# Re-searching a static instruction order with lengths measured from the trace

## The chip, the cores and the metric

The kernel runs on one core of one Trainium2 chip. The metric is device time in microseconds (us) of one execution. Three runs of the kernel before gave 1224.88, 1224.0 and 1226.82 us, median 1224.88. A profiled execution has a span of 1222.5 us from its first instruction to its last.

The engines are named as in the profile: PE multiplies matrices (PEld is its weight load), DVE and ACT do elementwise work, reductions and activations, POOL does slower elementwise work, SP only issues transfers. Each engine takes its instructions strictly in the order in which the program lists them, and waits where an operand or a buffer is not there yet. So the order in each engine's list decides how much of one engine's latency lies beside another's work.

## The reference

A random-feature attention for 8 batches of 8 heads is followed by a Fourier-mixing block with a two-layer network, all in float32:

```python
def phi(x):                                    # q and k, scaled
    h = einsum('bhsd,md->bhsm', x, omega) - sum(x*x)/2
    return exp(h - max(h)) / sqrt(m)
kv  = einsum('bhsm,bhsd->bhmd', k_p, v)        # per head: 128 features x 64
out = (q_p @ kv) / (q_p @ sum(k_p) + 1e-6)     # 8 x 8 heads x 576 x 64
x   = out as (8, 576, 512)
u   = x + real(fft(fft(x, axis=1), axis=2))
un  = (u - mean(u)) / sqrt(var(u) + 1e-6)
y   = u + relu(un @ w_ch1) @ w_ch2             # 512 -> 2048 -> 512
```

The two weight matrices come as 64-bit floats; the kernel converts them on the chip.

## The kernel before

The program has two parts. The first does the attention (32 pairs of heads, each a stream of steps), the Fourier mixing of eight batches, the conversion of the weights in 32 slabs, and the network for the first four tiles of 128 rows ("plain"). The second does the network for the other 4096 rows in eight blocks of 512, with a scheme that saves products by adding blocks first.

Neither part is written in its final order. Each stream is a generator that yields a `Step` before it emits the instructions of that step. A step names its engine (or a choice of two), an assumed length, events that it needs and makes, and buffers that it takes and gives:

```python
RATE = 190.0      # KB per us of a transfer
HOP = 0.15        # from the end of a step to its reader on another engine
TURN = 0.1        # change of PE's array mode (whole, quarters, halves)

class Listing:
    def run(self, streams, picks=None):
        ...
        for item in todo if pick is None else [todo[int(pick, 36)]]:
            got = self.start(*item[2:])             # earliest begin, by the assumed lengths
            key = got[0] + item[2].bias, item[0]
            if best is None or key < best[0]:
                best = key, got, item
        ...
        end = begin + step.engines[eng]
        done = end + step.late + (HOP if eng != NONE else 0.0)
        if step.kb:
            self.moved = max(self.moved, end) + step.kb / RATE
```

The first part is run with `PICKS`, a string of 1919 characters: each says which of the waiting streams goes next. It was found by a search outside the kernel. The second part is run without picks: there the step that can begin first, by the assumed lengths and a small bias, goes next. Where a step has a choice of engines, the assumed lengths decide in both parts. All of this happens when the program is built; on the chip there is only the resulting list of each engine.

The steps of one pair of heads (attention), by their lines in this kernel:

```python
def attn(n):
    # L470  PE: transpose k,q (9 tiles)         -> L477 ACT: copy out (kqT)
    # L544  PE: projection, 64x64 quarters      -> L488 DVE: negated maximum (nmx)
    #                                           -> L505 ACT: exp, 18 x 128x128 (e)
    # L578  PE: kv product (36, quarters)       -> L592 DVE or L594 ACT: copy out (kv)
    # L470  PE: transpose e of q (9 tiles)      -> L477 ACT: copy out (qeT)
    # L621, L629  PE: numerator and denominator (20, halves)
    # L638-L641   DVE: add, reciprocal, multiply -> x
```

The mixing of a batch folds x (L668 to L694, DVE, some on POOL), multiplies with cosine and sine tables (L712, then L739 and L744 on PE), and adds the residual (L760 ACT, L765 to L777 DVE and POOL). A slab of weights goes through:

```python
def narrow(i, dst, raw):
    step = Step({ACT: 0.72, POOL: 1.4}, ...)      # L407 POOL or L409 ACT: scale
    yield Step(DVE, 0.43, port=True, bias=0.19)   # L411
    yield Step(DVE, 1.15, port=True, bias=0.36)   # L413, L416
    yield Step(DVE, 0.7, port=True, bias=-0.99)   # L418
    yield Step(POOL, 1.3, makes=("w", i), ...)    # L420
```

The plain network is L863 (transposes of the normalised tile), L924 (first layer), L910 or L908 (relu on ACT or DVE) and L947 (second layer, added up by L960). It needs converted weights and mixed batches, so it is the work that can fill PE's gaps once both are there. In the second part L1130 is the first layer, L1309 the second; w2 is summed beforehand by L1017, w1 by L1075.

Of the kernel before, what the change touches and what calls it, by code (L numbers as in the profile page):

```python
# [33 lines left out]
PE, ACT, DVE, POOL, SP, NONE = "pe", "act", "dve", "pool", "sp", "none"  # L34
# [3 lines left out]
RATE = 190.0  # L38
HOP = 0.15

TURN = 0.1
# [7 lines left out]
    "00e2ede0ebed3dedebfcdcddfeede3fdfhbi8cdefdebfdgafaggec9hddk0kiij2jejgj7lfffffhcdfffdfcggjehegfi7gjbl"  # L49
    "hbhkjgkkdihfhi7hci7bfiadgkhhjce9didbhhb7gggbfihbbf97acbhbeghefaie8bc7chhhcgfc7cedddh9dd1ccdfif8eggih"  # L50
    "f6g8ejihichdihidfkhfhgjckgigh6eihggiddebd6dcg9eei7cfhei6ddfgihhj78gmkmiidaggjfigdmlg6khhjcj6agghifgg"
    "kh6afejekjkjfigji6j8hjjjiilcj9iegcigdhllkmldjmkkf9j80lca5m7bdai6gfikjaljkika6lhjggic9feikeejhgjij5d7"
    "ldjeafedkdeikjje5g5ielfafej6egkicg8dffgikghjijiee7eeifaaeefhefehdeh7iffd6hb7eeidiedhggiijbkj35fjkjhk"
    "kfgfhkk3h795g4e4i6khchlijigkjji4hlfjfd8lfhlg4mi64bfgjjedjgibk6ijj5cgcijhicgi6lii9fi9lf6ggdijf6bgd8fe"
    "icddchifajihj9fgihgjgi6jbhi6degcbg48ffgfh6ii5kjigihf7jgf9ejggafji7gf7egdfh6ficd6dbhfeeh5addfh5be5bff"
    "c48gai8hg9ageefcj5j7gh6haeeghhjikiehi5mg6lghhl5jjhagd5nglkmlccnjldj9llj45lkjjaemh6gbmlf8f7hgekef6hke"
    "87cldljj8bkhihbhhdc6ffgadkdf7ad5kdbgjhhig6lgcel5mdjedilaidedejihgjegi5ggjhcf5dgc5c775kccdh489j8ddgff"
    "h8cbdgiejkkechjhkkki5gj7kgjjjjfjjjh4i7dhhjjfi4k4h4kjchehg6ihk975g5bfejcehg3dgmggiej6m55bf9igig5h66gg"
    "jjjfiieifh8ege5kdihdlhiheief9k5fimhmcio8hgk7fge5jhgdeifagbgbjeeekhgclgigh7ge8fgefddfaci4icdffhgfid8f"
    "gjffhgihd6gc6cjeelgf3af8hbiccgchgfebg5c9d6ehdfcfeeagghffbhc6f9egchggh6aeehfeekjccbdfafdf50h0gcgabgea"  # L60
    "7fcdcfabg6be8bd4c9dcdcdbcebe6bcgb6cefbacadfeaca7dcdcdchdf9abca66f8dcbd8b98c8aa9c8dd2eabcc87a7b758697"
    "a27277ba9688848aa89a99992b98aa9a287a888729d8a993ba8ac9788aede65bdaacb69ba8ba659b54387a986aaa9baccade"
    "ad9b7bfcecffffde79fe9e6h9bgc3gc3be1eac26e7ebeddbdfeefegd6cdfed2ddf3dadeb3e3cc9dc6c5dbbdcab7b3c72b79b"
    "acbb8abbb679a6a9bb9ab49c7b38a93caa998888888888899888686981458778888888888888841933648786583b59691776"
    "a7c67267761bb4bcb6cc9a679a8aaba3f94df49cbaa675793a9aa88778388a88a93995aa39b94a4954585536126424112222"
    "3333533555523346545266421330442216087635433437704543770334535754155544556455155414437756241426224444"
    "1112032232202111100"
# [39 lines left out]
class Listing:  # L107
# [24 lines left out]
    def start(self, step, ready, before):  # L132

        queued = before in step.engines and len(step.engines) == 1
        t = ready[0] if queued else ready[1]
        for ev in step.after:
            if ev not in self.made:
                return None
            t = max(t, self.made[ev])
        for name in set(step.take):  # L140
            if name in WIDTH:
                t = self.banks_at(WIDTH[name], t)[1]
                if t == math.inf:
                    return None
                continue
            free = sorted(self.buffers[name])
            n = step.take.count(name)
            if len(free) < n:
                return None
            t = max(t, free[n - 1])  # L150

        def begin(e):
            return max(t, self.free[e] if e != NONE else 0.0, self.free[PORT] if step.on_port(e) else 0.0)

        eng = min(step.engines, key=lambda e: begin(e) + step.engines[e])
        t = begin(eng)
        return t + (TURN if eng == PE and step.mode != self.mode else 0.0), eng

    def run(self, streams, picks=None):
# [17 lines left out]
        while todo:  # L177
# [20 lines left out]
            done = end + step.late + (HOP if eng != NONE else 0.0)  # L198
# [55 lines left out]
def kernel(  # L254
# [142 lines left out]
    def narrow(i, dst, raw):  # L397


        lo, hi = raw[:, :, 0], raw[:, :, 1]  # L400
        lof, hif, bits = lo.bitcast(F32), hi.bitcast(F32), dst.bitcast(U32)


        step = Step({ACT: 0.72, POOL: 1.4}, after=(("raw", i),), port=True, bias=1.11)
        yield step
        if step.eng == POOL:
            nc.gpsimd.tensor_scalar(dst, hif, 2.0**-112, None, op0=ALU.mult)  # L407
        else:
            nc.scalar.activation(out=dst, in_=hif, func=AF.Copy, scale=2.0**-112)  # L409
        yield Step(DVE, 0.43, port=True, bias=0.19)  # L410
        nc.vector.tensor_scalar(hi, hi, 0x80000000, None, op0=ALU.bitwise_and)  # L411
        yield Step(DVE, 1.15, port=True, bias=0.36)
        nc.vector.scalar_tensor_tensor(  # L413
            bits, bits, 3, hi, op0=ALU.logical_shift_left, op1=ALU.bitwise_or
        )
        nc.vector.tensor_scalar(hi, bits, 0xFF800000, None, op0=ALU.bitwise_and)  # L416
        yield Step(DVE, 0.7, port=True, bias=-0.99)
        nc.vector.scalar_tensor_tensor(lof, lo, 2.0**-52, hif, op0=ALU.mult, op1=ALU.mult)  # L418
        yield Step(POOL, 1.3, makes=("w", i), give=("slab",), port=True, bias=1.25)
        nc.gpsimd.tensor_tensor(out=dst, in0=dst, in1=lof, op=ALU.add)  # L420
# [23 lines left out]
    def first():  # L444

        yield Step(NONE, 3.0)
        yield Step(PE, 0.4, take=("bank",))
        b, omps = got()
        nc.tensor.transpose(omps[:, 0:128], om[:].rearrange("m i d -> m (i d)"), ident[:])
        yield Step(DVE, 0.3, makes="om2", give=(b,))  # L450
        nc.vector.tensor_scalar(om2[:], omps[:, 0:128], SCALE, None, op0=ALU.mult)

    def transposed(src, name, groups, after, makes, give, back=None):
# [3 lines left out]
        for j0, j1 in groups:  # L457
# [3 lines left out]
                0.11 * m,  # L461
# [12 lines left out]
    def evicted(dst, b, j0, j1, makes, back):  # L474
        yield Step(ACT, 0.15 + 0.115 * (j1 - j0), 0.1, makes=makes + (j0,), give=(b,), bias=0.08)
# [5 lines left out]
    def softmax(n, ts, num, b, es):  # L481
# [3 lines left out]
        yield Step(DVE, 0.15 + 0.27 * num, bias=-0.56)  # L485
# [10 lines left out]
        for i, one in enumerate(b):  # L496
            if num == 4 or not i:
                yield Step(
                    ACT, 1.18 if num == 4 else 0.65, 0.0, take=(size,),
# [12 lines left out]
    def attn(n):  # L512
# [16 lines left out]
        def pairs_of(js, *ts):  # L529
# [4 lines left out]
                0.235 * len(js),  # L534
# [52 lines left out]
        def keep():  # L587
            step = Step({DVE: 0.3, ACT: 0.35}, take=("kv",), give=(kvb,), makes=("kv", n))
# [20 lines left out]
            1.23,  # L609
# [24 lines left out]
        yield Step(DVE, 1.25, after=(("frame", b),), give=(ndb,), makes=("x", b, pr), bias=-0.07)  # L634
# [18 lines left out]
    def mix(b):  # L653
# [7 lines left out]
        def folds(n):  # L661
            op = (ALU.add, ALU.subtract)[n]
            even, odd = (ALU.subtract, ALU.add) if n else (ALU.add, ALU.subtract)
            step = Step({DVE: 1.22, POOL: 2.5} if n else DVE, 1.22, take=("half",), port=True)
# [4 lines left out]
            yield Step(DVE, 1.15, port=True, bias=-0.08)  # L669
# [3 lines left out]
            for dst, src in ((h[:, 0:NL], h[:, 0:NL]), (h[:, NL : NL + 1], x[:, 4:5])):  # L673
# [7 lines left out]
                {DVE: 1.2, POOL: 2.6} if n else DVE, 1.2,  # L681
# [18 lines left out]
        for n, (tab, name) in enumerate(((cs, "cs"), (cs, "cs"), (sn, "sn"), (sn, "sn"))):  # L700
# [19 lines left out]
            def kept(n=n, yb=yb, yp=yp):  # L720
                yield Step(ACT, 0.44, 0.1, makes=("y", b, n), give=(yb,), bias=0.1)
# [3 lines left out]
        for c in range(NC3):  # L725
# [3 lines left out]
                1.33,  # L729
# [23 lines left out]
    def residual(b, c, x, abb):  # L753
# [3 lines left out]
        yield Step(ACT, 0.4, 0.1, take=("bmp",), give=(b1,))  # L757
# [4 lines left out]
        for last, (dst, op) in enumerate(((mi, ALU.subtract), (pl, ALU.add))):  # L762
            yield Step(DVE, 0.67, give=(b0,) if last else (), bias=-0.1)
# [23 lines left out]
        yield Fork(summed(0, mi, pl, DVE, 0.85))  # L787
        if c < NL:
            yield from summed(1, pl, mi, POOL, 1.6)
# [54 lines left out]
    def norm_of(j, t, i, pool, dst):  # L844
# [7 lines left out]
        yield Step(DVE, 1.09, bias=-0.23)  # L852
# [3 lines left out]
        yield Step(POOL, 0.7, port=True, bias=-0.18)  # L856
        nc.gpsimd.tensor_tensor(rstd[:], rstd[:], mhalf[:], op=ALU.pow)  # L857
        yield Step(DVE, 0.56, port=True)
        nc.vector.tensor_scalar(u[:], u[:], mv[:, 0:1], rstd[:], op0=ALU.subtract, op1=ALU.mult)
        yield Step(PE, 0.45, take=("bank",), give=("u",))  # L860
# [5 lines left out]
        yield Step(ACT, 0.6, 0.1, give=(b,), makes=("unT", j, i), bias=0.33)  # L866
# [25 lines left out]
    def plain_of(j):  # L892
# [4 lines left out]
        def hidden(fc, b, hp):  # L897
            step = Step(
                {ACT: 0.15 + TP / 1130.0, DVE: 0.15 + TP / 945.0},
                late=0.1,  # L900
# [12 lines left out]
        for fc in range(NFC):  # L913
            yield Step(
                PE,
                8 * TP / 1193.0,
# [38 lines left out]
    def rest(t, b, yp):  # L955
# [3 lines left out]
        yield Step(DVE, 0.7, after=(("op", t),), give=(b,), bias=1.38)  # L959
# [16 lines left out]
    def block_norms(j, pool):  # L976
# [13 lines left out]
        for i, (o, l, r, op) in enumerate(ops):  # L990
            yield Step(DVE, 0.7, makes=("tt", j) if i == 3 else None, port=True, bias=-0.49)
# [6 lines left out]
    def w2_parts():  # L998
# [14 lines left out]
        def op(o, l, r, **kw):  # L1013
            step = Step({DVE: 0.7, POOL: 1.35}, port=True, **kw, bias=-0.63)
# [47 lines left out]
    def weight_sums(groups):  # L1062
        yield Step(NONE, after=("converted",))
        for g in groups:
# [6 lines left out]
            for i, (o, l, r, op) in enumerate(ops):  # L1071
                yield Step(DVE, 0.7, makes=("w1s", g) if i == 3 else None, port=True)
# [45 lines left out]
    def first_of(j, fc):  # L1118
# [22 lines left out]
        def save(name, ps):  # L1141
            yield Step(ACT, 0.37, 0.1, take=("s",), makes=(me, name), bias=-2.15)
# [4 lines left out]
        def added(name, o, ps, with_, give, after=()):  # L1147
            yield Step(DVE, 0.42, 0.1, after=((me, with_),) + after, makes=(me, name), give=give, bias=1.96)
            relu_sum(o, ps[:, 0:HT], saved[with_][:])

        mm = 8 * HT / 1193.0 / 2
# [29 lines left out]
        yield Step(ACT, 0.37, 0.1, give=(xb,), makes=(me, "c21"), bias=0.73)  # L1181
# [4 lines left out]
            0.75,  # L1186
# [7 lines left out]
        for i, (o, l, r, op) in enumerate(ops):  # L1194
            if i:
                yield Step(POOL, 0.75, makes=("hs", j, fc) if i == 3 else None, port=True, bias=0.56)
# [53 lines left out]
    def product_of(j, i, cells):  # L1250
# [15 lines left out]
        def add_up():  # L1266
# [6 lines left out]
            for o, l, r, op, n in ops:  # L1273
                after = ready(0, 1) + ((me, "p5 read"),) * (n == 3)
                yield Step(DVE, 0.7, after=after, makes=(me, "s", n), port=True, bias=-0.39)
# [5 lines left out]
        def save(what, ps):  # L1281
            yield Step(ACT, 0.26, 0.1, take=("s",), makes=(me, what))
# [4 lines left out]
        def added(what, t, m, ps, with_, give):  # L1287
            yield Step(DVE, 0.28, 0.1, after=((me, with_),), makes=(me, what), give=give, bias=-1.15)
# [52 lines left out]
        yield Step(ACT, 0.26, 0.1, give=(xb,), makes=(me, "c21"))  # L1341
# [3 lines left out]
        def plus(o, other, **kw):  # L1345
            step = Step({POOL: 1.35, DVE: 0.7}, port=True, **kw, bias=0.06)
# [100 lines left out]
```

## Time and profile before

| what | value |
|---|---|
| median of 3 runs | 1224.88 us |
| span of the profiled execution | 1222.5 us |
| PE busy | 1188.2 us (97%) |
| PE weight loads busy | 1064.3 us (87%) |
| DVE busy | 746.0 us (61%) |
| ACT busy | 458.2 us (37%) |
| POOL busy | 383.5 us (31%) |
| granted TensorE clock | 0.997 |

The page's second part shows busy tenths of each engine in 40 equal slices, here for three engines:

```profile
PE   6989899999999999999999999999999999999997
DVE  4889899897674664384384285185276266267255
ACT  6867767666653521222222212222222222222211
```

A digit is the busy share of a slice of 30.6 us in tenths; 9 is 90% or more. The first part is roughly the first fifteen slices. The ends of matmuls are modelled in the profile, so short waits can hide in PE's busy time.

### The profile page before, as it was taken

The page shows a single profiled execution, that of the slowest core. Times are in us where ns is not written, and L with a number is a line of the kernel's source. Part 1 is how long each engine was busy: PE and PEld are TensorE (multiplying, and loading weights), DVE is VectorE, ACT ScalarE, POOL GpSimd, SP SyncE. Part 2 cuts the span into 40 slices and gives each one's busy share as a digit, 9 for nine tenths or more (in the row PEclk, how much of TensorE's full clock was granted, in tenths as well). Part 3 has the DMA queues.
Part 4 walks back from the last instruction along what each step waited for, and adds up shares of the span by engine and source line. Part 5 has one row for each costly group of instructions (what it writes and reads, how often), then busy time and mean ns, then how long its engine had stood idle before and what let it go on. Part 6 is the DMA issues. An engine that isn't in the chain of part 4 may idle for free.

```text
span 1222.5 us, 31614 instructions
## 1 busy us (share of the span) xinstructions
PE 1188.2 (97%) x12705; PEld 1064.3 (87%) x12705; DVE 746.0 (61%) x1522; ACT 458.2 (37%) x1432; POOL 383.5 (31%) x451
## 2 busy tenths in 40 slices
PE   6989899999999999999999999999999999999997
PEld 5778878878878777999899899899899899899897
DVE  4889899897674664384384285185276266267255
ACT  6867767666653521222222212222222222222211
POOL 3443443531111013322422422431431521431421
PEclk9999999999999999999999999999999999999999
DMA  9564654736653334195196096186186277267255
GB/s 262 155 205 146 200 177 144 218 91 210 175 194 130 123 114 162 55 304 168 35 304 188 10 309 186 30 284 193 50 258 201 59 248 218 61 212 255 61 175 172
DMA packets 149058, 206.02 MB, mean 169 GB/s; under 512 B 49328, under 2 KB 62896, under 8 KB 148912
## 3 DMA queue, kind: packets, MB, share of 16 engines
q1 hardware_dynamic: 144224, 187.15, 49.8%
q0 software_dynamic: 4608, 16.78, 4.3%
q8 instruction: 101, 1.65, 0.6%
q14 instruction: 45, 0.37, 0.1%
q10 hardware_dynamic: 80, 0.07, 0.0%
HBM read 172.23 MB, written 35.91 MB: 170 GB/s over the span
## 4 chain that ended last, share of the span: by engine, by line
PE 92%; DVE 3%; ACT 3%; DMA 0%; issue 0%; SPq 0%; DVEq 0%; ACTq 0%
PE banks L1130 32%; PE banks L1309 29%; PE banks L924 5%; PE banks L947 5%; PE banks L470 4%; PE banks L544 4%; PE banks L712 4%; PE banks L578 3%; PE banks L621 3%; ACT e L505 2%; PE banks L739 2%; PE banks L863 1%; DVE nmx L488 1%; PE banks L744 1%; ACT kqT L477 1%; PE banks L629 1%
## 5 line engine op out<-in xcount | busy, mean ns | idle before, releaser
L1116 DVE CUSTOM_DVE_ANT_0 hid<-banks,s 128x256 f32<-128x256 f32 x192 | 79.7, 423 | 254.9 <-PE banks L1130 254.9
L1309 PE MATMUL banks<-wl,sums 128*128 128x128 f32 x1792 | 220.3, 275 | 0.0
L1309 PEld LDWEIGHTS banks<-wl,sums 128*128 128x128 f32 x1792 | 210.5, 192 | 1.0
L505 ACT ACTIVATE e<-banks,nmx 128x128 f32<-128x128 f32 x576 | 158.9, 396 | 42.4 <-DVE nmx L488 42.4
L1144 ACT ACTIVATE s<-banks 128x256 f32<-128x256 f32 x192 | 73.6, 383 | 257.6 <-PE banks L1130 257.6
L1130 PE MATMUL banks<-unT,w 128*128 128x256 f32 x704 | 167.3, 379 | 0.0
L1130 PEld LDWEIGHTS banks<-unT,w 128*128 128x128 f32 x704 | 132.7, 190 | 17.9 <-issue 0.5
L1284 ACT ACTIVATE s<-banks 128x128 f32<-128x128 f32 x168 | 46.5, 277 | 236.9 <-PE banks L1309 175.5
L1130 PE MATMUL banks<-tt,w1s 128*128 128x256 f32 x512 | 126.3, 379 | 0.0
L1197 POOL TENSOR_TENSOR hs<-hid 128x256 f32<-128x256 f32 x64 | 46.4, 726 | 200.2 <-DVE hid L1116 173.6
L1130 PEld LDWEIGHTS banks<-tt,w1s 128*128 128x128 f32 x512 | 97.2, 190 | 13.3
L488 DVE TENSOR_REDUCE nmx<-banks 128x8 f32<-128x1024 f32 (+1 forms) x96 | 88.3, 953 | 32.2 <-PE banks L544 27.2
L1309 PE MATMUL banks<-wl,hid 128*128 128x128 f32 x768 | 98.9, 275 | 0.0
L1309 PEld LDWEIGHTS banks<-wl,hid 128*128 128x128 f32 x768 | 94.0, 192 | 1.4 <-DMA wl<-w2l 0.2
L1289 DVE TENSOR_TENSOR part<-banks,s 128x128 f32<-128x128 f32 x168 | 48.7, 290 | 75.3 <-PE banks L1309 74.2
L1197 POOL TENSOR_TENSOR hs<-hid,hs 128x256 f32<-128x256 f32 x64 | 46.4, 725 | 118.7 <-issue 93.3
L544 PE MATMUL banks<-om,kqT 64*64 64x128 f32 x2304 | 76.8, 275 | 4.7 <-ACT kqT L477 2.0
L1130 PE MATMUL banks<-unT,w1s 128*128 128x256 f32 x320 | 80.7, 379 | 0.0
L544 PEld LDWEIGHTS banks<-om,kqT 64*64 64x64 f32 x2304 | 63.8, 134 | 16.1 <-issue 4.2
L857 POOL TENSOR_TENSOR rstd<-rstd,mhalf 128x1 f32<-128x1 f32 x36 | 29.0, 806 | 153.6 <-DVE rstd L855 137.8
L1309 PE MATMUL banks<-wl,hs 128*128 128x128 f32 x576 | 74.9, 275 | 0.4 <-DVE part L1289 0.4
L420 POOL TENSOR_TENSOR w<-w,raw 128x512 f32<-128x512 f32 x32 | 43.7, 1367 | 99.5 <-DVE raw L418 80.5
(115 smaller groups left out, 1998.1 us busy)
## 6 DMA issues: line engine op xcount, KB each, us to landing
wl<-w2l SPq DMA_DIRECT2D x392, 256.0 KB, 3.7
raw<-in_moe_w_ch_dram POOLq DMA_DIRECT2D x32, 512.0 KB, 5.2
kq<-in_k_dram SPq DMA_DIRECT2D x32, 288.0 KB, 3.8
kq<-in_q_dram SPq DMA_DIRECT2D x32, 288.0 KB, 4.5
vd<-in_v_dram SPq DMA_DIRECT2D x32, 288.0 KB, 4.9
out_dram<-ur SPq DMA_DIRECT2D x68, 128.0 KB, 2.4
u<-us SPq DMA_DIRECT2D x32, 256.0 KB, 4.0
ur<-us SPq DMA_DIRECT2D x32, 256.0 KB, 3.1
```

The source lines that it names most:

```text
L470: nc.tensor.transpose(ps[:, (j - j0) * 128 : (j - j0 + 1) * 128], src(j), ident[:])
L488: nc.vector.tensor_reduce(nmx[:, :, 0:num], pps[:, :, 0 : MF * num].rearrange("p b (c m) -> p b c m", m=MF), axis=AX.X, op=ALU.max, negate ...
L505: nc.scalar.activation(out=e[:, c + (i if num == 1 else 0), :], in_=pps[:, i, MF * c : MF * c + MF], func=AF.Exp, bias=nmx[:, i, c : c + 1],)
L544: nc.tensor.matmul(pps[cols, c, MF * m : MF * m + MF], lhsT=kqT[rows, j, cols], rhs=om2[rows, :],)
L712: nc.tensor.matmul(yp[:, 0:NK], lhsT=fold[:, c, n, :], rhs=tab[:, c, :], start=(c == 0), stop=(c == NC3 - 1),)
L924: nc.tensor.matmul(hp[:, 0:TP], lhsT=w1[:, dc, 128 * fc : 128 * fc + 128], rhs=unTs[key][:, dc, :], start=(dc == 0), stop=(dc == NDC - 1),)
L947: nc.tensor.matmul(yp[:, 0:DM], lhsT=hs[fc][:, 128 * i : 128 * i + 128], rhs=w2[:, fc, :], start=(fc == 0), stop=(fc == NFC - 1),)
L1116: nc.vector._custom_dve(TENSOR_ADD_SAT, out=o, in0=ps, in1=sb, s0=FMAX, s1=0.0)
L1130: nc.tensor.matmul(ps[:, 0:HT], lhsT=left(dc), rhs=right(dc), start=start and dc == 0, stop=(dc == D2 - 1), skip_group_check=True,)
L1144: nc.scalar.activation(out=s[:], in_=ps[:, 0:HT], func=AF.Copy)
L1197: nc.gpsimd.tensor_tensor(out=o, in0=l, in1=r, op=op)
L1309: nc.tensor.matmul(ps[:, 0:128], lhsT=left[:, f], rhs=wls[j, i, n][:, f], start=start and f == 0, stop=(f == 3), skip_group_check=True,)
```

## The change

The constants are set anew from what a trace of the kernel showed: transfers at 270 instead of 190 KB per us, a hop of 0.036 instead of 0.15 us, and, new, a tail for each engine (from the end of its occupation to the end that others see) and a lead ahead of a PE step. The length of nearly every step is set anew. With this model the picks of the first part were searched again, and the whole string is replaced. The second part has no picks; its order follows from the new lengths. The computation, the tiles and the buffers stay as they were. The core of the diff, cut:

```diff
-RATE = 190.0
-HOP = 0.15
-
-TURN = 0.1
+RATE = 270.0
+HOP = 0.036
+LEAD = 0.2
+TURN = 0.06
+TAIL = {PE: 0.163, ACT: 0.105, DVE: 0.085, POOL: 0.02, SP: 0.0, NONE: 0.0}
 PICKS = (
-    "00e2ede0ebed3dedebfcdcddfeede3fdfhbi8cdefdebfdgafaggec9hddk0kiij2jejgj7lfffffhcdfffdfcggjehegfi7gjbl"
+    "00e2de0eadae3dddddae3bbddfddg9bhghaigf0gggg9fcchha98adciddijcd2jddcbcbbc7ggggceeabedae7fddecbeeedece"
     ... (19 lines, all replaced)
-        queued = before in step.engines and len(step.engines) == 1
-        t = ready[0] if queued else ready[1]
+        queued = before in step.engines and before in (PE, SP, NONE)
+        t = 0.0 if queued else ready[1]
     ...
+        if PE in step.engines:
+            t += LEAD
+        if queued:
+            t = max(t, ready[0])
     ...
-            done = end + step.late + (HOP if eng != NONE else 0.0)
+            done = end + step.late + TAIL[eng] + (HOP if eng != NONE else 0.0)
     ...  weights
-        step = Step({ACT: 0.72, POOL: 1.4}, after=(("raw", i),), port=True, bias=1.11)
+        step = Step({ACT: 0.57, POOL: 1.55}, after=(("raw", i),), port=True, bias=1.11)
-        yield Step(DVE, 0.43, port=True, bias=0.19)
+        yield Step(DVE, 0.34, port=True, bias=0.19)
     ...  attention
-                0.11 * m,                                    # transposes
+                0.109 * m,
-        yield Step(DVE, 0.15 + 0.27 * num, bias=-0.56)       # maximum, num = 4, 1, 4
+        yield Step(DVE, 0.063 + 0.267 * num, bias=-0.56)
-                    ACT, 1.18 if num == 4 else 0.65, 0.0, take=(size,),
+                    ACT, 1.0 if num == 4 else 0.5, 0.04, take=(size,),
-                0.235 * len(js),                             # L544
+                0.23 * len(js),
     ...  mixing
-                1.33,                                        # L739, L744
+                1.52,
     ...  plain network
-                {ACT: 0.15 + TP / 1130.0, DVE: 0.15 + TP / 945.0},
-                late=0.1,
+                {ACT: 0.165, DVE: 0.2},
-                8 * TP / 1193.0,                             # L924
+                0.893,
     ...  second part
-            yield Step(ACT, 0.37, 0.1, take=("s",), makes=(me, name), bias=-2.15)
+            yield Step(ACT, 0.28, take=("s",), makes=(me, name), bias=-2.15)
-        mm = 8 * HT / 1193.0 / 2                             # L1130
+        mm = 0.864
     ...  (some thirty more lengths)
```

## The prediction

> **What bounds the kernel now.** I read three views in this order: the table of stages (busy time of each engine in each stretch of the span), the waits of the tensor engine, and the list of instruction groups. The stages, cut to the ones that matter (microseconds; busy time and, in brackets, instructions of PE, PE weight loads, DVE, ACT, POOL; then granted clock, DMA share, GB/s):
>
> ```profile
> 0.00:50.00 50.00, 37.74 (x970) 32.55 (x971) 30.17 (x49) 35.83 (x119) 17.06 (x26) 1.00 0.85 237
> 50.00:100.00 50.00, 44.47 (x957) 38.77 (x956) 44.25 (x87) 37.17 (x118) 22.63 (x21) 0.97 0.60 173
> 100.00:150.00 50.00, 45.48 (x921) 39.40 (x919) 45.42 (x91) 36.33 (x118) 21.06 (x21) 1.00 0.58 171
> 150.00:200.00 50.00, 45.94 (x924) 40.06 (x925) 46.64 (x97) 36.24 (x113) 19.35 (x18) 1.00 0.54 162
> 200.00:250.00 50.00, 49.59 (x889) 39.30 (x893) 44.39 (x86) 35.56 (x119) 25.53 (x24) 1.00 0.62 191
> ...
> 350.00:400.00 50.00, 50.00 (x585) 39.86 (x585) 30.89 (x70) 19.31 (x62) 8.64 (x9) 1.00 0.41 133
> ...
> 700.00:800.00 100.00, 100.00 (x681) 93.94 (x680) 53.95 (x111) 22.59 (x67) 32.61 (x41) 1.00 0.55 170
> ```
>
> The reader is to see two parts. From about 464 us (where the first matmul of L1130 stands in the timeline) PE is busy all the time and loads weights 94 us of each 100. Before that it is idle 12.3, 5.5, 4.5 and 4.1 us in the first four stretches of 50, 26.4 us in all, and 0.4 in the fifth. Between 50 and 200 us DVE is busy 88 to 93% and ACT 73 to 74%: DVE has hardly any room. The waits of PE say for whom it waits:
>
> ```profile
> PE banks L470 <- ACT e L505: 6.5, 7, 1.9
> PE banks L449 <- DMA om<-in_omega_dram: 3.5, 1, 3.5
> PE banks L578 <- ACT e L505: 3.2, 4, 1.4
> PE banks L470 <- DMA kq<-in_k_dram: 2.1, 1, 2.1
> PE banks L621 <- ACT e L505: 2.0, 1, 2.0
> PE banks L544 <- ACT kqT L477: 2.0, 4, 0.8
> PE banks L544 <- DVE x L641: 1.4, 3, 0.6
> ```
>
> (us in total, times, longest). Mostly for the exponentials of L505, which wait for DVE's maximum (L488). The first transfers (omega, first k and q) hold the first pair of heads until 7.9 us in the chain that ended last, and no order of instructions moves that.
>
> ```profile
> 7.88 1.30 PE banks L470 x5
> 9.18 1.96 PE banks L544 x32
> 11.16 1.24 DVE nmx L488
> 12.42 2.69 ACT e L505 x10
> ```
>
> **How much is there to win.** PE's work in the first part, by steps: the chain shows 0.893 us for four matmuls of L924 (7.14 for the eight-fold), 1.72 for a step of L947, 1.21 for one pair's L578, 3.23 for two of L712. With these, and the changed kernel's own lengths where the chain agrees with them (0.109 a transpose, 0.23 a position of L544, 1.22 for L621 with L629, 1.52 for L739 with L744), the sum is: transposes 576 x 0.109 = 62.8; L544 32 x 9 x 0.23 = 66.2; L578 32 x 1.21 = 38.7; L621 and L629 39.0; L712 32 x 1.62 = 51.8; L739 and L744 24 x 1.52 = 36.5; L924 64 x 0.893 = 57.2; L947 32 x 1.72 = 55.0; L863 8 x 0.437 = 3.5; L449 0.3; in all 411. The part lasts 464.2, of which 7.9 lie before the first transpose. So 464.2 - 7.9 - 411 = 45 us are waits and changes of mode. Only 20 of them (26.4 + 0.4 less 6.3 of idle time in the first 8 us) show as idle.
>
> The second part: one block is 56 steps of L1130 at 0.864, 49 of L1309 at 0.893 and four transposed tiles at 0.44, that is 48.4 + 43.8 + 1.8 = 93.9 us; the chain repeats every 94.05. There is nothing left in it to win, whatever its order.
>
> **What the Trainium skill says.** Perfetto Trace Analysis, section "Tensor Engine Instruction": the end of a matmul in the profile is computed, not observed. The trace agrees: L924's 512 records count 63.1 us of busy time, where the chain gives 57.2. So waits of a few tenths are counted as busy, which is why 45 and not 20 us are lost. The same page, "Identifying the Most-Contended Engine": weight-load time tells more than matmul time. Here 94% in the second part and 77 to 80% between 50 and 200 us, which says the same. The same page, "Optimizing Scalar/DVE Operations": the write-acknowledgement half of an instruction's latency overlaps with the next. The trace agrees: the maximum of L488 shows 1220 ns where the change books 0.063 + 4 x 0.267 = 1.13 us plus a tail of 0.085, and L411 shows 509 ns against 0.34. DVE's busy share is therefore above its real occupancy. SBUF — State Buffer, "Who interferes with whom": a DVE instruction with two SBUF inputs contends with a GpSimd instruction that reads SBUF. The trace agrees:
>
> ```profile
> L777 DVE TENSOR_TENSOR x<-x,bmp 128x255 f32<-128x255 f32 x16 | 14.7, 920 | 0.0
> L776 DVE TENSOR_TENSOR x<-x,bmp 128x257 f32<-128x257 f32 x16 | 7.4, 462 | 0.0
> ```
>
> (busy us, mean ns, idle before.) The same addition takes twice as long in the row that meets POOL's additions; both listings book the two engines as sharing a port.
>
> **The change, part by part.** No instruction is added or removed. (1) The list of picks, which fixes the first part's order on all five engines, is replaced. (2) The lengths change in the listing that orders the second part. (3) Choices of engine follow: the scaling of L409/L407 goes from 15 on ACT and 17 on POOL to 20 and 12 (ACT +5 x 0.57 = 2.9 us, POOL -5 x 1.55 = 7.8 us, neither the bound); one difference of the w2 sums goes from POOL to DVE (+0.6 us); one relu of L908 from DVE to ACT.
>
> The order of instructions in the two built programs gives the rest (lines are numbered as in the kernel before). On PE the runs of one kind of matmul in the first part fall from 335 to 317 and the changes of array mode (whole, quarters, halves) from 164 to 160: at the 0.06 us a turn that the change books, 0.2 us, with perhaps 1 us for the 18 shorter run ends. The start (rows up to the first kv product and the first e transposes) is the same, so the first 20 us stay.
>
> For the middle I counted, up to the k-th finished pair of heads, the work ahead of it in each engine's order. Before: at k = 8, 16, 24, 32 PE 67, 150, 255, 369 us and DVE 66, 148, 234, 305. After: PE 72, 144, 247, 353 and DVE 71, 137, 229, 302. In the kernel before, the 16th pair's result (L641) ends at 195.6 and the 32nd at 423.5. So of the 45 us lost, 195.6 - 7.9 - 150 = 38 are lost up to the 16th pair, where DVE has as much to do as PE, and about 8 later. The new order brings 11 us less DVE work and 6.5 us less PE work before the 16th pair: it puts weight conversions and matmuls of L924 later. And it leaves 59 instead of 42 us of PE work behind the last pair, where nothing waits. Against it: at the 12th pair DVE stands at 111 and PE at 107 (before 111 and 113), so there PE has to wait at least 3 to 4 us more than its own work.
>
> Loss up to the 16th pair: about 8 us are fixed (the first pair's chain from 11.1 to 17.3 us, and the first e's after it). The other 30 fall with the density of DVE work: I take a third off, because DVE's work drops by 11 in 148 and because the lengths by which the picks were searched now hold the tail and lead that the old ones lumped together. That is -10, and the 12th pair takes back +3. The turns give -1. In the later stretch 8 us are lost; with less slack between 16 and 24 (DVE 92 in 104, before 86 in 105) I take +1, and for the end -2. Sum: -10 + 3 - 1 + 1 - 2 = -9 us in the first part. Second part: 0 to -0.5.
>
> 1224.9 - 9.4 = 1215.5 us.
>
> **Rivals.** (a) The reordering is paid back: the waits move from the exponentials to DVE in the stretches 4 to 12, where the new order asks 84 us of DVE against 77 of PE (before 86 against 85). For it: DVE at 88 to 93%. Against it: the count runs together again by the 16th pair. It would make 1222 to 1228. (b) The order was good only in the model: real transfers come late, since the new rate of 270 GB/s is above the 237 that the first 50 us moved, and loads that were booked early stand behind others. For it: only the start, where 85% of the DMA engines' time is used. Against it: later stretches move 162 to 191 and the same two k/q buffers and three v buffers bound in both orders how far loads run ahead. It would cost 2 to 5 us: 1217 to 1220. (c) The search finds nearly all: the loss up to the 16th pair falls to 8 plus the turns, some 20 us gained: 1204. (d) The second part's new order breaks its steady state. The next block's four transposed tiles now stand after 13 and 24 leaf products of L1309 (two each) rather than after 17, 35 and 36; a wait of 1 us in each of seven blocks would cost 7. Against it: DVE has 46% and ACT 77% free there.
>
> **Range and chances.** The lower end lies just above (c), 1206; the upper end in the middle of (a), 1225. More than 2% faster is below 1200.4, which would need 24.5 of the 45 us, of which 8 are fixed and turns (160 x 0.06 = 10) cannot go: 0.03. More than 2% slower is above 1249.4, which only a stall that nothing here shows could bring: 0.02. The rest 0.95; I hold a gain of over 2 us for 80% likely.
>
> **What would show it.** The first matmul of L1130's kind at about 455 us instead of 464.1; idle PE up to 200 us down from 26.4 to some 18; the 16th pair's result at about 180 instead of 195.6; blocks of the second part still 94.05 apart. If the 16th pair comes no earlier than 190, the step on DVE's density is wrong; if it does and the first part still ends at 464, the waits have moved behind it, to the stretch from 16 to 24. If the gain is right but PE's idle time hardly moves, it lies in the short waits that the computed ends hide.

## The result, and the profile after

The changed kernel takes 1242.1 us (median of 4 runs, 1240.55 to 1242.91) against 1224.44 us before: a ratio of 1.0138, 95% interval 1.0124 to 1.0152. It is 17 us slower, where 9 us less were predicted. Single runs of the kernel before spread over 1222.9 to 1229.9 in the comparisons below, so each of them rests on its ratio and not on one time.

The stages of the changed kernel (columns as for the kernel before: us, then busy time and instructions of PE, weight loads, DVE, ACT, POOL, then clock, DMA share, GB/s):

```profile
0.00:50.00 50.00, 38.53 (x967) 32.64 (x968) 27.37 (x44) 36.01 (x120) 16.72 (x25) 1.00 0.82 227
50.00:100.00 50.00, 44.17 (x910) 38.06 (x911) 44.48 (x91) 37.44 (x122) 13.91 (x16) 0.94 0.55 163
100.00:150.00 50.00, 48.06 (x1019) 42.71 (x1012) 41.75 (x90) 37.36 (x121) 18.44 (x18) 0.99 0.62 186
150.00:200.00 50.00, 47.26 (x882) 39.64 (x882) 47.11 (x95) 37.90 (x124) 17.26 (x17) 1.00 0.57 173
200.00:250.00 50.00, 47.89 (x1058) 42.18 (x1060) 42.59 (x91) 38.97 (x127) 18.31 (x20) 1.00 0.65 191
...
700.00:800.00 100.00, 98.37 (x655) 91.60 (x654) 48.76 (x102) 22.39 (x67) 32.79 (x42) 1.00 0.53 164
```

Two things are to be seen. PE's idle time up to 200 us fell from 26.4 to 22.0 us, but between 200 and 250 it rose from 0.4 to 2.1 us. And the second part, which had no idle PE before, now has 1.6 us of it in each 100. The waits of PE, over the whole span and longest first, name a newcomer at the top:

```profile
PE banks L1314 <- DVE part L1294: 10.3, 8, 1.4
PE banks L476 <- ACT e L511: 4.1, 6, 1.5
PE banks L455 <- DMA om<-in_omega_dram: 3.3, 1, 3.3
PE banks L550 <- ACT kqT L483: 2.9, 4, 1.3
```

The first of them is in the second part (L1314 is L1309 of the kernel before, L1294 its L1289: DVE adds a product sum out of a bank that PE wants back). The chain that ended last shows the two places of a block where PE is held up:

```profile
612.31 10.73 PE banks L1314 x96
...
623.07 0.29 DVE part L1294
623.36 1.33 DVE u L865 x2
...
624.73 0.66 PE banks L869 x4
625.39 10.11 PE banks L1314 x88
...
640.06 0.29 DVE part L1294
640.35 1.46 DVE tt L997
641.81 0.89 DVE sums L1281
...
643.40 0.68 DVE unT L997
644.08 0.60 DVE sums L1281
644.68 0.21 DVE part L1294
...
644.94 10.98 PE banks L1314 x96
```

At 623.04 two transposes (L869) need the normalised rows (L865), which stand on DVE behind a product sum. From 637.28 on the products need a bank that a product sum frees only at 644.9. PE meanwhile works on what its list has ahead, so what it loses is less than the stretch of the chain: before 644.94 it stands idle for 1.42 us. The kernel before runs the same stretch on PE alone:

```profile
608.45 15.18 PE banks L1309 x136
623.63 0.87 PE banks L863 x8
624.50 16.25 PE banks L1309 x144
```

A block takes 96.3 us instead of 94.05 (669.83 to 766.18 in the chain). Seven blocks repeat, so 7 x 2.3 = 16 us come from here. In the chain the first matmul of L1135 (the former L1130) begins at 465.7 instead of 464.3 us: of the 18.5 us between the two spans (1222.5 and 1241.0) 1.4 lie in the first part and 17.1 in the second.

### The profile page after: what moved, and what is told of

Its sections match the earlier page's. It is cut to its first block, busy times and chain, and to the rows that moved or that the text cites. A ratio compares the mean times of both kernels' runs of the same rounds, so it can differ in the third digit from the quotient of the medians.

```text
span 1241.0 us, 31565 instructions
## 1 busy us (share of the span) xinstructions
PE 1196.6 (96%) x12705; PEld 1067.9 (86%) x12705; DVE 733.0 (59%) x1524; ACT 456.4 (37%) x1438; POOL 367.2 (30%) x443
## 4 chain that ended last, share of the span: by engine, by line
PE 82%; DVE 10%; ACT 3%; DMA 2%; issue 2%; SPq 0%; DVEq 0%; ACTq 0%
PE banks L1135 31%; PE banks L1314 24%; PE banks L952 5%; PE banks L929 4%; PE banks L550 4%; PE banks L718 4%; PE banks L476 3%; PE banks L584 2%; ACT e L511 2%; DVE sums L1281 2%; PE banks L627 2%; DMA u<-us 2%; PE banks L745 1%; PE banks L869 1%; DVE tt L997 1%
## 5 line engine op out<-in xcount | busy, mean ns | idle before, releaser
L1314 PE MATMUL banks<-wl,sums 128*128 128x128 f32 x1792 | 219.2, 276 | 10.0 <-DVE part L1294 9.9
L1314 PEld LDWEIGHTS banks<-wl,sums 128*128 128x128 f32 x1792 | 209.4, 192 | 12.5 <-DVE part L1294 11.3
L1135 PE MATMUL banks<-unT,w 128*128 128x256 f32 x704 | 167.4, 379 | 0.0
L1135 PEld LDWEIGHTS banks<-unT,w 128*128 128x128 f32 x704 | 131.6, 190 | 17.0 <-issue 0.5
L1289 ACT ACTIVATE s<-banks 128x128 f32<-128x128 f32 x168 | 46.6, 277 | 238.2 <-PE banks L1314 211.8
L1135 PE MATMUL banks<-tt,w1s 128*128 128x256 f32 x512 | 126.4, 379 | 0.0
L1294 DVE TENSOR_TENSOR part<-banks,s 128x128 f32<-128x128 f32 x168 | 48.7, 290 | 109.5 <-PE banks L1314 108.5
L1135 PEld LDWEIGHTS banks<-tt,w1s 128*128 128x128 f32 x512 | 97.1, 190 | 13.4
L1314 PE MATMUL banks<-wl,hid 128*128 128x128 f32 x768 | 100.6, 276 | 0.0
L1314 PEld LDWEIGHTS banks<-wl,hid 128*128 128x128 f32 x768 | 94.6, 192 | 1.6 <-DVE part L1294 0.2
L1135 PE MATMUL banks<-unT,w1s 128*128 128x256 f32 x320 | 80.7, 379 | 0.0
L426 POOL TENSOR_TENSOR w<-w,raw 128x512 f32<-128x512 f32 x32 | 41.2, 1289 | 130.4 <-DVE raw L424 123.5
L550 PEld LDWEIGHTS banks<-om,kqT 64*64 64x64 f32 x2304 | 66.5, 138 | 13.5 <-ACT kqT L483 5.5
L863 POOL TENSOR_TENSOR rstd<-rstd,mhalf 128x1 f32<-128x1 f32 x36 | 25.1, 698 | 165.9 <-DVE rstd L861 165.9
L1314 PE MATMUL banks<-wl,hs 128*128 128x128 f32 x576 | 72.6, 275 | 0.4 <-DVE part L1294 0.4
```

The lines of the kernel that those rows point to most:

```text
L550: nc.tensor.matmul(pps[cols, c, MF * m : MF * m + MF], lhsT=kqT[rows, j, cols], rhs=om2[rows, :],)
L1135: nc.tensor.matmul(ps[:, 0:HT], lhsT=left(dc), rhs=right(dc), start=start and dc == 0, stop=(dc == D2 - 1), skip_group_check=True,)
L1294: nc.vector.tensor_tensor(out=part[:, t, 128 * m : 128 * m + 128], in0=ps[:, 0:128], in1=saved[with_][:], op=ALU.add,)
L1314: nc.tensor.matmul(ps[:, 0:128], lhsT=left[:, f], rhs=wls[j, i, n][:, f], start=start and f == 0, stop=(f == 3), skip_group_check=True,)
```

## The experiments

All are edits of one kernel in which each part can be ordered by either model: with both old it is the kernel before, with both new the changed one. Line numbers of these kernels are shifted against both.

**1 and 2. One part at a time.**

```diff
+    M.update(FIRST)      # new model and new picks / model and picks of before
     listing = Listing(buffers)
     ...
+    M.update(SECOND)     # model of before / new model
     listing.run([late_norms(), halves(), loads_w2(), weight_sums((1, 2, 3))])
```

> The first part in the new order, the second in the order of before. Theory S (the second part's new order is what costs: seven blocks at 96.3 instead of 94.05 us are 16 us): blocks back at 94.05, time 1225 to 1227, 1 to 2 us above before. Theory F (the first part's order delays what the second part needs, so its blocks stay slow): 1238 to 1243.

> The first part in the order of before, the second in the new one. Theory S: 1239 to 1242, blocks at 96.3 us. Theory F: blocks at 94.05, time 1224 to 1226.

Measured: the new first part alone 1223.46 us, ratio 0.998 (0.9969 to 0.9992), blocks at 94.04 us. The new second part alone 1244.75 us, ratio 1.0156 (1.0141 to 1.0171), blocks at 96.3. Theory S holds for the second part; the first part came out 2.4 us below the kernel before by its ratio, where the theory had 1 to 2 above. The two effects, 2.4 us less and 19 us more, multiply to 1.0136, the whole of the change. The first part's search did gain: some 2 us.

**3 and 8. Why a product sum is late.** DVE's list ahead of the sum that PE waits for, and POOL's list, in the changed kernel's second block:

```profile
640.06 0.29 DVE L1294 TENSOR_TENSOR part<-banks,s 128x128 f32<-128x128 f32 x1
640.26 1.54 DVE L997 TENSOR_TENSOR tt<-unT,tt 128x512 f32<-128x512 f32 x1
641.73 1.75 DVE L1281 TENSOR_TENSOR sums<-hs 128x512 f32<-128x512 f32 x1
643.40 0.68 DVE L997 TENSOR_TENSOR unT<-unT 128x512 f32<-128x512 f32 x1
644.01 0.68 DVE L1281 TENSOR_TENSOR sums<-sums,hid 128x512 f32<-128x512 f32 x1
644.61 0.28 DVE L1294 TENSOR_TENSOR part<-banks,s 128x128 f32<-128x128 f32 x1
```

```profile
639.45 3.49 POOL L1354 TENSOR_TENSOR ur<-ur,part 128x512 f32<-128x512 f32 x2 [6.90 <-ACT part L1347]
```

Two of DVE's additions take 1.54 and 1.75 us, where their neighbours of the same shape take 0.68; just then POOL makes two additions in 3.49 us. The prediction's citation of the Trainium skill (SBUF — State Buffer, "Who interferes with whom") fits: all four read two SBUF operands.

```diff
-            eng = nc.gpsimd if step.eng == POOL else nc.vector
-            eng.tensor_tensor(out=o, in0=o, in1=other, op=ALU.add)
+            if step.eng == POOL:        # run 3; leaves the addition out
+                return
+            nc.vector.tensor_tensor(out=o, in0=o, in1=other, op=ALU.add)   # run 8: always on DVE
```

> As the second run (first part of before, second part new), but the some 23 additions of product results that the listing gave to POOL are left out; every other list stays as it is. Theory P (POOL's two long additions hold the port that DVE's additions need; DVE's tt and sums take 1.5 and 1.75 instead of 0.7 us, 1.9 us in all, and the product sum that PE waits for stands behind them): the 1.4 us wait per block goes, the block falls to about 94.9, time about 1231. Theory Q (DVE's list simply has too much ahead of that product sum): blocks stay at 96.0 to 96.3, time 1238 to 1241.

> As the second run (first part of before, second new), with the 23 additions that the listing gave to POOL issued on DVE at the same places in the order. DVE gets 0.6 us for each instead of standing 1 us behind POOL's port. Theory P: blocks at about 95.0, time 1232 to 1236. Theory Q: blocks at 96.3 to 97.5, time 1243 or more.

Measured (run 2's order is the base, at 1.0156): without the additions 1233.11 us, ratio 1.0055 (1.0036 to 1.0073); with them on DVE 1235.3 us, 1.0081 (1.0058 to 1.0104); a block takes 94.9 us in both, from the distance of its transposes over four blocks. In run 3 the same two additions of DVE, a block later (L997 and L1281 are L1018 and L1303 there), take 0.68 us:

```profile
737.45 0.68 DVE L1018 TENSOR_TENSOR tt<-unT,tt 128x512 f32<-128x512 f32 x1
738.05 0.68 DVE L1303 TENSOR_TENSOR sums<-hs 128x512 f32<-128x512 f32 x1
```

Theory P holds: 1.4 of the 2.3 us a block come from POOL's additions beside DVE's. That only DVE's list were too long is excluded by run 8, where the list is longer and the block as short. What stays, 0.9 us a block, is the other stop, in run 3 as in the changed kernel (no run takes it away):

```profile
709.61 10.73 PE banks L1336 x96
720.34 0.02 issue
720.37 0.29 DVE part L1316
720.66 1.33 DVE u L886 x2
721.99 0.04 issue
722.03 0.66 PE banks L890 x4
722.69 10.00 PE banks L1336 x88
732.69 0.87 PE banks L890 x8
733.56 17.87 PE banks L1336 x160
```

The next block's tiles are transposed after 13 products now, and their normalisation (L886) waits in DVE's list behind a product sum. The second stop is gone: 160 matmuls, 20 products, run on.

**11, 12, 14 and 15. Which constant spoils the order.** The first part is that of before in all four.

```diff
-SECOND = {'len': 1, 'rule': 1, 'tail': 1, 'rate': 1}
+SECOND = {'len': 1, 'rule': 0, 'tail': 0, 'rate': 0}     # run 11: lengths alone
+SECOND = {'len': 0, 'rule': 0, 'tail': 1, 'rate': 0}     # run 12: hop, tails, lead, turn alone
-                key = got[0] + item[2].bias, item[0]
+                key = got[0] + (item[2].bias if M["bias"] else 0.0), item[0]   # runs 14, 15: no bias
```

> First part of before; in the second part only the lengths of the steps are new, not hop, tails, lead, rate and the rule of what is queued. If the lengths (0.6 for 0.7 of a DVE addition, 0.205 for 0.28 of a product sum) are what turns the order bad: blocks at 95.5 us or more, 1236 or more. If not: blocks at 94.05 to 94.5, 1225 to 1228.

> First part of before; in the second part only hop, tails, lead and turn are new. If these turn the order bad: blocks at 95.5 us or more. If not: 94.05 to 94.5, 1225 to 1228.

> First part of before. In the second part the lengths of before, but all biases zero. Theory B (the order of before is good because its biases were tuned to its lengths, and the new lengths came without new biases): blocks over 95 us, 1233 or more. If the old lengths are good by themselves: blocks at 94.05 to 94.3, 1224 to 1228.

> First part of before. In the second part the new model, all biases zero. Theory B: no worse than the new model with the old biases, blocks at most 96.3, and nearer to the fourteenth run than the two are with biases. If the new lengths are bad by themselves: blocks at 96.3 or more, and over 1 us above the fourteenth run's.

| second part | us | ratio, 95% | block | what PE waits for most, from 470 us on |
|---|---|---|---|---|
| lengths new, rest old | 1242.4 | 1.013, 1.0112 to 1.0149 | 96.3 | ACT s, 7.4 us |
| hop, tails, lead, turn new, rest old | 1237.1 | 1.0086, 1.0068 to 1.0105 | 95.6 | DVE sums, 6.4 us |
| all old, no bias | 1242.5 | 1.014, 1.0112 to 1.0167 | 96.6 | DVE sums, 4.6 us |
| all new, no bias | 1243.7 | 1.0149, 1.0119 to 1.0179 | 96.1 | DVE u, 8.3 us |

(Blocks again from the transposes.) Each order waits for something else, and none is at 94.05. The old lengths are not good by themselves: without their biases they give 96.6. With the biases they give 94.05; the new model with the same biases gives 96.3, no better than with none (96.1). So Theory B holds: what was good was the pair of lengths and biases. The change set the lengths anew and kept the biases, and the part without picks lost an order that only the pair gave. Each of the four kernels ran twice, so their blocks carry this reading and not the 1.2 us between the last two times. How the biases had been found is not on record; that they were tuned against the old lengths is the likely reading. The new rate alone and the new rule for queued steps alone were not run, and that new biases would bring 94.05 back with the new lengths was not tried.

**4 and 5. Choices of engine in the first part.** Run 4 has the picks of before with the new lengths; run 5 has the new picks with all scalings of weight slabs on POOL. (The string of picks has 1819 characters in both kernels, not 1919.)

```diff
-    PICKS (new)                        # run 4: those of before, FIRST = new model
-        if step.eng == POOL:           # run 5
+        if True:
             nc.gpsimd.tensor_scalar(dst, hif, 2.0**-112, None, op0=ALU.mult)
```

> The picks of before, with the new lengths choosing engines and banks in the first part; second part as before. PE's order is then that of before but for three lines; what moves is which of ACT, DVE and POOL takes the steps that have a choice. Theory C (these choices are what the first part loses): 1226 to 1230. Theory D (they do not matter, the order of the picks does): within 1 us of before.

> As the first run (first part new, second of before), with the 20 scalings of weight slabs that the listing gave to ACT issued on POOL, at the same places: 11.4 us of work leave ACT, 31 us come to POOL. Theory A (the first part's remaining loss is ACT's: PE waits for the exponentials): 6 to 9 us less, about 1215 to 1218. Theory V (it is DVE's): no gain, and DVE loses to POOL at the shared port: 1223 to 1227.

Measured: run 4 1232.73 us, 1.0058 (1.0041 to 1.0075). It put 28 of 32 scalings and all 32 copies of kv on ACT (before 15 and 22); ACT is busy 468.4 instead of 458.2 us. Run 5 1229.47 us, 1.0039 (1.0024 to 1.0053), against 0.998 with 20 on ACT and 12 on POOL. Theory C holds for run 4, by more than its numbers. Run 5 goes against Theory A, and lies above what V gave too. Both extremes cost some 7 us, run 4 against the kernel before and run 5 against run 1. So the split matters; that picks are good only with the choices that they were searched with is the likely reason, but it is argued here and not shown (run 4 also moves banks, and run 5 gives POOL more than it takes from ACT).

**6, 7, 9 and 10. What holds the first part.** Work is taken off ACT, off DVE, and off both; the outputs then lack what is left out.

```diff
-            for c in range(num):        # runs 6, 9, 10: one exponential per bank, three maxima unused
+            if num == 4:
+                nc.scalar.activation(out=e (all 512), in_=pps[:, i, 0:512], func=AF.Exp, bias=nmx[:, i, 0:1])
+                continue
-        nc.vector.tensor_scalar(hi, hi, 0x80000000, ...)            # runs 7, 9, 10: the conversion's
-        nc.vector.scalar_tensor_tensor(bits, bits, 3, hi, ...)      # four DVE instructions left out
-        nc.vector.tensor_scalar(hi, bits, 0xFF800000, ...)
-        nc.vector.scalar_tensor_tensor(lof, lo, 2.0**-52, hif, ...)
-        nc.gpsimd.tensor_tensor(out=dst, in0=dst, in1=lof, op=ALU.add)
+        nc.gpsimd.tensor_tensor(out=dst, in0=dst, in1=hif, op=ALU.add)
```

> As the first run, with one exponential over a bank's four column blocks instead of four, which leaves out the maxima of three of them: some 2 us less ACT work for each of the 32 pairs, 67 us in all, no other list changed. Theory A: the loss up to the 16th pair falls by over 10 us, time at most 1213. Theory V: less than 4 us gained, 1220 or more.

> As the first run, with the four DVE instructions of each weight slab's conversion left out: 2.1 us less DVE work for each of 32 slabs, 68 us in all, most of it before 250 us. Theory V: over 10 us gained, at most 1213. Theory A: less than 5 us gained.

> As the first run (first part new, second of before), with both the four DVE instructions of each slab's conversion and three of four exponentials per bank left out: 68 us less on DVE and 67 us less on ACT. Theory M (ACT and DVE each suffice to make PE wait, so that cutting one alone shows nothing): at most 1213. Theory I (the rest of the loss is PE's own: its instruction supply, stalls of 2 to 4 us in the middle of a group behind no dependency, and turns): 1217 or more.

> The same two cuts in the kernel before. Theory M: at most 1210. Theory I: 1217 or more, and within 5 us of the same cuts with the new picks.

| kernel | us | ratio, 95% |
|---|---|---|
| new first part (run 1) | 1223.46 | 0.998, 0.9969 to 0.9992 |
| run 6: one exponential per bank | 1222.96 | 0.9977, 0.9965 to 0.999 |
| run 7: no conversion on DVE | 1227.1 | 1.0006, 0.9996 to 1.0016 |
| run 9: both | 1222.65 | 0.9973, 0.9962 to 0.9985 |
| run 10: both, order of before | 1224.36 | 0.9988, 0.9978 to 0.9999 |

Theories A, V and M all fall. Against run 1, ACT is busy 52 us less in run 6 (405.4 us) and DVE 63 us less in run 7 (674.1 us), less than the 67 and 68 us by the assumed lengths; in run 9 the two together lose 115 us, and the time moved by 1 us. Theory I (the rest is PE's own) stands. In the trace the waits for ACT shrink as they should (up to 470 us from 13.6 in run 1 to 6.4 us in run 6), and stalls without any dependency come in their place. PE's timeline in run 6:

```profile
84.58 1.14 PE L607 MATMUL banks<-vd,e 64*64 64x65 f32 x58
89.25 0.70 PE L607 MATMUL banks<-vd,e 64*64 64x65 f32 x14 [3.53 <-issue]
```

Here PE stops for 3.5 us after 58 of 72 records of one group, and no operand is new in the rest. Run 6 has 8.7 us of such stalls, run 7 5.6, run 9 9.3 us, the kernel before 0.2 and the changed one 1.2.

**13 and 16. What the stalls hang on.**

```diff
-                nc.gpsimd.dma_start(raw[:].rearrange("p n two -> p (n two)"), src.bitcast(U32))
+                nc.gpsimd.dma_start(raw[:, 0:128]..., src[:, 0:128].bitcast(U32))
-        lo, hi = raw[:, :, 0], raw[:, :, 1]
+        lo, hi = (raw[:, 0:128, i].unsqueeze(1).to_broadcast([128, 4, 128]) for i in (0, 1))
```

Only a quarter of each weight slab is moved (12.6 of 16.8 MB are left out) and read four times. Run 13 is run 9 with this edit, run 16 is run 7 with it.

> As the ninth run (both cuts, new picks), with only a quarter of each weight slab transferred and used four times: 12.6 MB of 16.8 are left out, nearly all before 250 us, the instructions stay. Theory I with transfers (PE's stalls behind no dependency are its own instructions' transfers standing behind data transfers): the stalls called issue fall from 9 us to under 3, time 1212 to 1217. If they are PE's own pace: they stay at 7 or more, 1220 to 1223.

> As the thirteenth run (a quarter of each weight slab transferred, DVE's conversion left out), but with all four exponentials per bank again: ACT has its 67 us back. If PE's waits for the exponentials count once transfers no longer hold its instructions: 1217 to 1221, 4 to 8 us above the thirteenth run. If they do not count even then: within 2 us of it.

Measured: run 13 1212.77 us, 0.9896 (0.9878 to 0.9914), 10 us below run 9; run 16 1217.26 us, 0.9945 (0.9926 to 0.9964). PE's waits behind no dependency, first in run 9, then in run 13:

```profile
PE banks L644 <- issue: 3.6, 1, 3.6
...
PE banks L567 <- issue: 3.1, 3, 1.7
PE banks L601 <- issue: 2.6, 2, 2.2
```

```profile
PE banks L649 <- issue: 2.0, 1, 2.0
...
PE banks L572 <- issue: 1.6, 1, 1.6
...
PE banks L606 <- issue: 0.4, 1, 0.4
```

They fall from 9.3 to 4.0 us, less far than the expected 3; from run 7 to run 16 they fall from 5.6 to 0.9 us. So they hang on the load of the DMA engines.

What PE waits for there can be read from the traces: its own instructions. The page lists a DMA queue of its own kind, "instruction", with 101 packets and 1.65 MB, 16 KB each. Its packets can be set beside the stalls. In run 6 PE stands from 85.73 to 89.25 us; a packet of this queue sets out at 87.02 and lands at 87.98. In run 9 PE stands from 23.78 to 27.36; the packet sets out at 24.80 and lands at 26.09. All 34 stalls of this kind over 0.3 us in the first part, in the 18 traces, end 1.2 to 1.6 us after such a landing (a moment taken at random between 10 and 240 us lies so behind one in some 7% of cases), and counted in matmuls and weight loads of PE they lie a multiple of 256 apart, give or take one. The Trainium skill (Runtime: NRT & Kernel Launch, "Instruction fetch mechanics") describes such blocks of 16 KiB, 256 instructions, and calls the cost of crossing from one to the next "mostly hidden"; here, with ACT's or DVE's work left out, it was not.

The packets are not slow: 0.96 and 1.29 us in the two cases, with a median of 1.0 over run 9. They set out late, beside 16 engines that data keep busy 80 to 88% in the first 50 us of these runs. What makes them set out late no run isolates. Nor are all of the 10 us between runs 9 and 13 such stalls: PE's idle time up to 470 us falls by 7.4 us, 5.3 of it these stalls and 1.5 waits for operands that land sooner.

Run 16 shows that ACT's waits do count here: with the exponentials back the time rises by 4.5 us, 6 by the ratios. But lighter transfers are not what makes them count. Runs 7 and 9, with all transfers, differ in the same exponentials, and from 1.0006 to 0.9973 are 4 us. With DVE's conversion in place, between runs 1 and 6, it was 0.4 us. So what hid them in run 6 is DVE's work, which runs 7, 9, 13 and 16 all leave out.

## Why the prediction was wrong

**Second part.** The term "Second part: 0 to -0.5" failed, and with it "nothing left in it to win, whatever its order", which saw only half: a part with no slack on PE can lose. Run 2 measured +19 us, 16 of them seven times 2.3 us a block. One stop stood there as rival (d), in the right place (transposes after 13 and 24 products) and well sized at 1 us a block, for 0.9 measured; it was set aside because "DVE has 46% and ACT 77% free there". The larger one, 1.4 us at a product sum, was in no rival, although the prediction named its cause, POOL's additions beside DVE's, for another line. The share of free time is an average over the block; in the 7.5 us from 637.3 on DVE is busy for 7.46, and two of its additions take more than twice their time. The order shown by the two programs said that the products' place had moved; asking which DVE instructions stand ahead of which product sum would have shown the rest.

**The first part's gain.** -9 us were predicted, run 1 measured -2.4 (interval of the ratio: 0.8 to 3.1 thousandths, 1.0 to 3.8 us). The step "the other 30 fall with the density of DVE work: I take a third off" failed. The 16th pair's result did come early, at 185.0 us for a predicted 180 or so: 6.5 us of that is less PE work ahead of it, and 185.0 - 7.9 - 143.5 = 33.6 us of loss instead of 38 is 4.4 us of the -10. What the prediction named as the sign of this case then happened: the loss behind the 16th pair rose from 8 to 465.7 - 185.0 - 267.5 = 13 us, and PE's idle time between the 16th and the 24th pair from 0.4 to 3.4 us. And DVE's density is not what sets the loss: in run 7, with DVE busy 63 us less, the time did not fall (1.0006, against 0.998 in run 1).

**The reading of the waits.** Most idle time was put down to ACT's exponentials, as the waits named them. That was the last arrival, not the only one: with ACT's and DVE's work cut, PE's waits for its own instructions took the same place (runs 6, 7, 9 and 10).

**What held.** The first 20 us stayed (8.8 us of idle PE before, 8.3 after), and the 16th pair came early. PE's work of 411 us is a sum that no run puts to the test. What the prediction set aside without need were the choices of engine ("neither the bound"): runs 4 and 5 show 7 us between one split and another.

The first part of the change with the second part of before, run 1, is the version that beats both kernels: the one before by 0.2%, the changed one by some 1.5% (1223.46 and 1242.1 us).

## What to carry to other kernels

When the constants of a scheduler are corrected, everything that was tuned against the old ones (biases, picks, choices of engine) should be searched again, in every part that uses them, and the part left alone should be timed by itself: here lengths read from a trace cost 1.6% in the part that was not searched again (run 2). A part whose critical engine is saturated is the one to check first, because it can only lose. And before work is taken off the engine that a wait names, find out by leaving it out whether the wait goes or only changes its name.

## What the runs showed of the hardware

PE stalled for up to 3.7 us in the middle of a group of small matmuls because its own instructions came late: every such stall over 0.3 us in the first part ended 1.2 to 1.6 us after a 16-KB packet of the instruction queue had landed, and the stalls were fewer with fewer bytes moved (9.3 to 4.0 us, and 5.6 to 0.9).

A DVE addition of 128x512 with two SBUF operands took 1.54 and 1.75 us beside POOL's additions, and 0.68 without them (run 3).

The granted clock dropped once or several times between 10 and 150 us, at different places in runs of one order. In the kernel before the stretch from 72.47 to 75.88 us reads 0.50; in run 3, which has the same first part, 74.74 to 81.56 and 139.59 to 143.00. So a drop was to half clock, for 3.4 us or twice that, which is the window and the step that the Trainium skill gives (TensorE: Matmul & The Clock Gate, "What's actually happening"). In the changed kernel's profile 93.74 to 100.57 us reads 0.50, which is 3.4 us of full clock lost, against 1.7 in that of the kernel before: single profiles of the first part compare no better than that. Some drops go with the stalls: in runs 6 and 9 half clock set in within 0.8 us of the end of four of the five stalls over 2 us (47.60 us beside 47.77, 88.56 beside 89.25; 27.74 beside 27.36, 89.18 beside 88.46). In the 3.41 us ahead of the drops PE was busy for 1.42 us in the kernel before and for 1.99 us in the changed one.
